# Moving transposed attention weights between partitions by DMAs through DRAM, in three vector operations a step and not in twelve

## The chip, the cores and the metric

The kernel runs on one core of a Trainium2 chip. The metric is the time of one execution on the device in microseconds (us), lower is better. Before the change the median of three runs is 905.54 us (904.55 to 905.82). Engines are named as in the profile: PE is TensorE (PEld its weight loads), DVE is VectorE, ACT is ScalarE, POOL is GpSimd, SP is SyncE, which here issues DMAs.

## The reference

Attention within a band of 64 keys, for 8 batches, 8 heads, 576 positions and 64 numbers a head, then a feed-forward layer over the 4608 tokens:

```python
scores = scale * np.matmul(q, k.transpose(0, 1, 3, 2))
mask = (rel >= 0) & (rel < window)          # rel = query - key, window = 64
scores = np.where(mask, scores, -1000000000.0)
attn = np.exp(scores - np.max(scores, axis=-1, keepdims=True))
attn = attn / (np.sum(attn, axis=-1, keepdims=True) + 1e-09)
x = np.matmul(attn, v)                      # then heads side by side: 4608 x 512
h = x @ w_in                                # 512 x 2048
g = np.where(h >= 1, h, np.where(h <= -1, 0.0, (h + 1) ** 2 / 4))
out = g @ w_out                             # 2048 x 512
```

## The kernel before

**Tiles and steps.** The tokens are worked off in nine tiles of 512. A tile's attention is four steps of 128 queries (steps 4t to 4t+3; from tile 2 on they are done in the order first, third, second, fourth, so step 8, 10, 9, 11). A step of the later kind is, for all eight heads at once: scores on PE (L409, 32 queries against the 96 keys that they can see), scale and mask on DVE (L426), maximum on DVE (L430), exponential on ACT (L437), sums turned over on DVE (L444, L445), division on DVE or POOL (L449), transposition of the weights on DVE (L455 in `att_transpose_both`), and the product with the values on PE (L484, `att_values`). Some steps' scores and an earlier step's values are issued as one piece.

**Why the transposition has twelve parts.** DVE transposes blocks of 32 x 32. The scores of 32 queries cover 96 keys, in three blocks of 32 columns. The product with the values needs keys on partitions, and the keys of the four groups of 32 queries start at different partitions; so each of 4 groups x 3 blocks is an operation of its own that reads 32 partitions and writes 32 others. The result lies in `ptd`, a buffer of which steps from `SOON` = 8 on use one copy (`pt2`): the next step's transpositions wait until this step's L484 is done. Steps below 8 do it in other ways (L464, or on PE by L470) and don't change.

**The feed-forward layer.** Weights are split in a high and a low part, and each product is made of three. Tiles 0 and 1 use the plain form: L873 for `x @ w_in` (groups of twelve matmuls for 128 columns of `w_in`), gates on ACT and DVE (L885, L890, L897, ACT L902, POOL L907), L924 for the second product (groups of twelve). From tile 2 on (`PLAIN`) the first product is formed from sums and differences of operand blocks, as L824, in chunks n = 0 to 7 of a tile with 24 and then 18 matmuls; DVE puts the pieces together (L840). It needs sums of the weights, which are made once during tile 1 on DVE and POOL (L734, L743, L753; ACT L265) and stored to DRAM (`kept`, L723, L758, L759), and from there loaded for each chunk into two pairs of ring buffers (`wr`, L796). It also needs sums and differences of a tile's x (the "build", two a tile: the copy L267 or L265 into `u`, four L537, five pairs of a rounding and L549).

**What sets the order.** `Plan` holds every piece of work with a key, a cost for each engine that may do it, what it comes after, and the buffers that it takes and gives back. It works through a timeline of its own: on each engine the piece that can start takes the next place, the lowest key first, and the instructions are issued in that order. So a changed cost or piece moves work on all engines. On the chip each engine works through its list in order and waits where a piece isn't ready. All loads and stores are issued by SP, in its list's order: ring loads, queries (`qt`), keys (`kt`), values (`vt`, four buffers), stores of sums and of the result (`out`, L955).

Of the kernel before, what the change touches and what calls it, by code (L numbers as in the profile page):

```python
# [10 lines left out]
F32 = mybir.dt.float32  # L11
F32R = mybir.dt.float32r
# [8 lines left out]
P = 128  # L21
QB = 64
SB = 2 * QB
WIN = 128
WINDOW = 64
SQ = 32
NEAR = WINDOW + SQ
# [12 lines left out]
SOON = 8  # L40
# [60 lines left out]
R_LEAD = 6  # L101
R_LOAD = 2800, 2100
A_EARLY = 5


class Plan:
# [87 lines left out]
def banded_attention_then_ffn(ctx: ExitStack, tc: tile.TileContext, q, k, v, w, masks, out, dims):  # L194
    nc = tc.nc
    B, H, S, D = dims
    NT, DM = out.shape
    NP = H // 2
# [25 lines left out]
    nmsk = const.tile([P, 3, WIN], F32, name="nmsk")  # L224
    idr = const.tile([P, P], F32R, name="idr")
    mskr = const.tile([P, 3, WIN], F32R, name="mskr")
    wpool = ctx.enter_context(tc.tile_pool(name="wpool", bufs=1))
    dram = ctx.enter_context(tc.tile_pool(name="dram", bufs=1, space=bass.MemoryType.DRAM))
    kept = [dram.tile([P, 2, 2, 7, P], F32, name=f"kept{n}") for n in range(NF // 2)]


    for n, at in ((P, QB), (QB, 0)):
        m = msk[:n, 0]
# [9 lines left out]
        nc.gpsimd.tensor_copy(msk[:, n], msk[:, 0])  # L243
        nc.gpsimd.memset(msk[r, n, :QB], NEG)

    ptq = const.tile([P, BUFS["ptd"], NP, SB], F32, name="ptd")
    ptd = [ptq[:, i] for i in range(BUFS["ptd"])]
    for t in ptd:
        nc.vector.memset(t, 0.0)

# [9 lines left out]
    add = plan.add  # L260
# [101 lines left out]
    blk, vals = {}, {}  # L362
    qts, kts, vts, pts = {}, {}, {}, {}
    starts = [sum(TILES[:t]) for t in range(len(TILES))]
    half = [slice(0, D), slice(D, P)]

    def pt_of(s, h):
        return h if s >= SOON else (2 * seq[s] + h) % len(ptd)

    def variant(s):  # L370
        firsts = [(2 * s + i) % NB == 0 for i in range(2)]
        return 1 if firsts[0] else 2 if firsts[1] else 0

    def near(s):
        return s >= PE_STEPS
# [12 lines left out]
        nc.sync.dma_start(out=t, in_=v[b * QB:b * QB + WIN])  # L388

    def load_masks():  # L390
        nc.sync.dma_start(out=nmsk[:, :, :NEAR], in_=masks)

    def round_masks():
        nc.scalar.copy(idr, idt)
        nc.scalar.mul(mskr[:, :2], msk[:, :2], 1.0 / scale)

    def att_scores(s, masked, pool):
        qt, kt = qts.pop(s), kts.pop(s)
# [21 lines left out]
    BOTH = slice(0, 2)  # L420

    def att_masked(s, h):
        ps, sm, _, _ = blk[s, h]
        m = nmsk[:, variant(s), :NEAR] if near(s) else msk[:, variant(s)]
        m = m.unsqueeze(1).broadcast_to(sm.shape)
        nc.vector.scalar_tensor_tensor(out=sm, in0=ps, scalar=scale, in1=m, op0=ALU.mult, op1=ALU.add)  # L426

# [20 lines left out]
        _, sm, _, den = blk[s, h]  # L448
        engine[eng].tensor_tensor(out=sm, in0=sm, in1=den.unsqueeze(2).broadcast_to(sm.shape), op=ALU.mult)  # L449

    def att_transpose_both(s, i, j, c):
        r = slice(i * QB + j * SQ, i * QB + (j + 1) * SQ)
        src = blk[s, BOTH][1][r].rearrange("p h a n -> p (h a) n")
        dst = ptq[(c + j) * SQ:(c + j + 1) * SQ, :2].rearrange("p h a n -> p (h a) n")
        nc.vector.transpose(dst[:, :, r], src[:, :, c * SQ:(c + 1) * SQ])  # L455

    def att_transpose(s, h, i):

# [15 lines left out]

    def att_values(s, pool):

        vt, pt = [vts.pop((s, i)) for i in range(2)], [ptd[pt_of(s, h)] for h in range(2)]
        vals[s] = ps = banks_of_heads(pool)
        for p in range(NP):
            for i in range(2):  # L480
                n = slice(i * QB, (i + 1) * QB)
                for h in range(2):
                    c = (2 * p + h) * D
                    nc.tensor.matmul(  # L484
                        ps[half[h], p, n], lhsT=vt[i][:, c:c + D], rhs=pt[h][:, p, n], start=True, stop=True
                    )

    def att_high(t, i, eng):
# [64 lines left out]
    early_values = []  # L553
    x_ready, x_first, x_after, seq = {}, {}, {}, {}
# [30 lines left out]
    def add_step(t, i):  # L585
# [44 lines left out]
        if s < SOON:  # L630
            for h in range(2):
                x = xs
# [30 lines left out]
        else:  # L663
# [478 lines left out]
```

## Time and profile before

| | |
|---|---|
| median of three runs | 905.54 us (904.55 to 905.82) |
| the profiled execution | 907.99 us, its span 906.2 us |
| mean granted clock of PE in it | 0.987 |
| DMA packets in it | 108033, 187.60 MB |
| DVE, transposition L455 | 336 operations, 146.5 us |
| SP waiting to issue ring loads (L796 for L824) | 426.1 us in 108 waits |

The page of the profile gives for each engine the time in which it was busy. PE's matmuls overlap, so a mean duration of one is longer than the pace at which they follow each other; groups in the timeline or in the chain show the pace. A view by stretches gives the busy times between two points in time, the view of waits who waited for whom (total, times, longest), the timeline the instructions of an engine in order, where [a <-b] is idle time ahead of a row and what ended it. The part of DMA issues gives the size of one and the median time from issue to landing.

### The profile page before, as it was taken

Reading aid. Unit: us, or ns where it says so; the run is one execution under the profiler, and the core shown is the slowest. Engines: PE = TensorE matmul, PEld = TensorE weight load, DVE = VectorE, ACT = ScalarE, POOL = GpSimd, SP = SyncE. Lnnn points to the kernel's source line nnn. Section 1 sums busy time; section 2 is a strip of 40 time slices with the busy share of each in tenths; the row PEclk is TensorE's granted clock in tenths of the full one; section 3 lists DMA queues with packets and bytes.
Section 4 is the critical chain, followed back from the end, with each engine's and each line's share of the span. In section 5 each row is a group of like instructions: output and inputs, shape, how many; then the busy total and the mean of one; then the engine's idle time right before and its main releaser. Section 6 shows DMA issues by size and latency. Waiting matters only on the chain.

```text
span 906.2 us, 20363 instructions
## 1 busy us (share of the span) xinstructions
PE 875.5 (97%) x7839; PEld 762.9 (84%) x7839; DVE 656.1 (72%) x1391; ACT 506.8 (56%) x1291; POOL 264.2 (29%) x268
## 2 busy tenths in 40 slices
PE   7699997999799999999999999999999999999998
PEld 5587885887688888888898889888988888899997
DVE  6999996598977868777686767676767676833331
ACT  7998863554455555655565537454655565434343
POOL 1000034455432232423142324232413242322222
PEclk9999996999899999999999999999999999999999
DMA  9991149447567666766676658666765664557531
GB/s 333 410 377 55 54 146 291 146 157 239 198 214 226 213 199 215 253 204 193 218 251 216 216 181 285 204 204 216 260 208 194 206 228 163 164 169 237 175 117 47
DMA packets 108033, 187.60 MB, mean 207 GB/s; under 512 B 8480, under 2 KB 49696, under 8 KB 107936
## 3 DMA queue, kind: packets, MB, share of 16 engines
q1 hardware_dynamic: 107648, 185.38, 60.9%
q8 instruction: 62, 1.02, 0.5%
q10 hardware_dynamic: 288, 0.92, 0.3%
q14 instruction: 35, 0.29, 0.1%
HBM read 162.15 MB, written 24.12 MB: 206 GB/s over the span
## 4 chain that ended last, share of the span: by engine, by line
PE 75%; DVE 12%; DMA 5%; ACT 3%; issue 2%; SPq 2%; POOL 0%; ACTq 0%; DVEq 0%
PE acc L924 36%; PE ps_h L824 27%; PE ps_h L873 6%; DVE ptd L455 4%; PE ps_a L484 3%; PE ps_a L409 3%; DVE a L897 2%; DMA kept<-half 2%; DMA kt<-in_k 2%; SPq L723 1%; ACT a L885 1%; DVE h L840 1%; DVE sm L449 1%; DVE half L734 1%; DVE half L743 1%
## 5 line engine op out<-in xcount | busy, mean ns | idle before, releaser
L924 PE MATMUL acc<-wts,gh 128*128 128x512 f32 x1154 | 363.2, 396 | 2.7 <-ACT o L265 2.7
L824 PEld LDWEIGHTS ps_h<-xs,wr 128*128 128x128 f32 x2352 | 294.5, 189 | 10.3 <-DVE h L840 0.7
L824 PE MATMUL ps_h<-xs,wr 128*128 128x256 f32 x2352 | 299.2, 282 | 0.3 <-DVE h L840 0.3
L907 POOL TENSOR_TENSOR gl<-a,gh 128x512 fp32r<-128x512 f32 (+1 forms) x130 | 167.6, 1290 | 427.5 <-ACT gh L902 389.7
L924 PEld LDWEIGHTS acc<-wts,gh 128*128 128x128 f32 x1154 | 207.9, 189 | 44.6 <-ACT o L265 3.4
L924 PE MATMUL acc<-wts,gl 128*128 128x512 f32 x577 | 225.9, 391 | 0.0
L840 DVE TENSOR_TENSOR h<-h,ps_h 128x256 f32<-128x256 f32 x280 | 117.5, 420 | 127.8 <-PE ps_h L824 113.0
L902 ACT CAST gh<-a 128x512 fp32r<-128x512 f32 (+1 forms) x149 | 90.0, 604 | 133.9 <-PE acc L924 112.2
L455 DVE STREAM_TRANSPOSE ptd<-sm 32x256 f32<-32x256 f32 x336 | 146.5, 436 | 6.3
L924 PEld LDWEIGHTS acc<-wts,gl 128*128 128x128 f32 x577 | 108.7, 188 | 23.9
L885 ACT ACTIVATE a<-h 128x512 f32<-128x512 f32 x112 | 69.9, 624 | 72.3 <-DVE h L840 71.4
L897 DVE SCALAR_TENSOR_TENSOR a<-a,h 128x512 f32<-128x512 f32 x112 | 85.7, 765 | 27.7 <-ACT a L890 16.2
L873 PE MATMUL ps_h<-xh,wts 128*128 128x512 f32 (+1 forms) x296 | 93.3, 385 | 10.7 <-DVE a L897 6.6
L437 ACT ACTIVATE sm<-sm,nm 128x96 f32<-128x96 f32 (+1 forms) x256 | 93.0, 365 | 12.2 <-DVE nm L430 12.1
L890 ACT ACTIVATE a<-a 128x512 f32<-128x512 f32 (+1 forms) x139 | 85.8, 617 | 4.3
L873 PEld LDWEIGHTS ps_h<-xh,wts 128*128 128x128 f32 x296 | 56.8, 200 | 22.6 <-DVE a L897 8.1
L873 PE MATMUL ps_h<-xl,wts 128*128 128x512 f32 (+1 forms) x148 | 56.3, 380 | 0.7 <-DVE xl L497 0.6
L265 ACT COPY h<-ps_h 128x256 f32<-128x256 f32 x77 | 28.7, 372 | 47.3 <-PE ps_h L824 43.6
L549 POOL TENSOR_TENSOR xs<-u,xs 128x256 fp32r<-128x256 f32 (+1 forms) x45 | 42.3, 971 | 32.0 <-ACT xs L265 32.0
L734 POOL TENSOR_TENSOR half<-wts 128x256 f32<-128x256 f32 x12 | 9.4, 790 | 140.1 <-PE ps_h L873 123.7
L437 ACT ACTIVATION_READ_ACCUMULATOR sm<-sm,nm 128x1 f32 x256 | 47.9, 187 | 0.0
L484 PEld LDWEIGHTS ps_a<-ptd,vt 128*64 128x64 f32 x992 | 32.0, 137 | 13.1 <-DVE ptd L455 3.6
(89 smaller groups left out, 728.3 us busy)
## 6 DMA issues: line engine op xcount, KB each, us to landing
wr<-kept SPq DMA_DIRECT2D x112, 512.0 KB, 4.7
wr<-kept SPq DMA_DIRECT2D x112, 384.0 KB, 3.9
vt<-in_v SPq DMA_DIRECT2D x72, 256.0 KB, 4.9
kt<-in_k SPq DMA_DIRECT2D x35, 384.0 KB, 5.4
raw<-in_w SPq DMA_DIRECT2D x12, 1023.8 KB, 10.3
qt<-in_q SPq DMA_DIRECT2D x36, 256.0 KB, 4.8
out<-o SPq DMA_DIRECT2D x33, 256.0 KB, 4.0
kept<-wts SPq DMA_DIRECT2D x48, 128.0 KB, 2.4
```

What stands on the lines that cost most here:

```text
L437: nc.scalar.activation(sm[:, p, :], (ps if masked else sm)[:, p, :], AF.Exp, bias=nm[:, p:p + 1], scale=scale if masked else 1.0, accum_ou ...
L455: nc.vector.transpose(dst[:, :, r], src[:, :, c * SQ:(c + 1) * SQ])
L484: nc.tensor.matmul(ps[half[h], p, n], lhsT=vt[i][:, c:c + D], rhs=pt[h][:, p, n], start=True, stop=True)
L824: nc.tensor.matmul(ps[:, c * 2 * SB:(c + 1) * 2 * SB], lhsT=r[:, part, cp, o], rhs=xo[k][:, xp, cp], start=i < 2 and c == 0 and j == 0 and ...
L840: nc.vector.tensor_tensor(out=h[:, to:to + 256], in0=h[:, of:of + 256], in1=ps[:, at:at + 256], op=ALU.add)
L873: nc.tensor.matmul(ps, lhsT=wts[f, 0][:, part, c * P:(c + 1) * P], rhs=x[:, c, r], start=(c == 0 and j == 0), stop=(c == NP - 1 and j == 2),)
L885: nc.scalar.activation(gs[t, f, r.start][0], phs[t, f, r.start], AF.Relu, bias=0.5, scale=0.5)
L890: nc.scalar.activation(a, a, AF.Square)
L897: nc.vector.scalar_tensor_tensor(out=a, in0=a, scalar=1.0, in1=ps, op0=ALU.min, op1=ALU.max)
L902: nc.scalar.copy(g[1], g[0])
L907: engine[eng].tensor_tensor(out=g[2], in0=g[0], in1=g[1].bitcast(F32), op=ALU.subtract)
L924: nc.tensor.matmul(acc[t, i][:, n], lhsT=g[:, sub], rhs=wts[f, 1][:, part, n], start=(q == 0 and j == 0), stop=(q == NF - 1 and j == 2 and ...
```

## The change

From step 8 on the weights are transposed by three operations over all 128 partitions, one for each block of 32 keys (`att_turn`), into `turned_at`: what comes out has, on partition 32g + k, the key k of block c of the query group g. One DMA writes that to a buffer in DRAM (`att_put`, 128 rows of 3 KB; `passed`, two of them, by the step's parity). Four DMAs, one for each group of 32 queries, read it back (`att_get`), each 96 rows of 1 KB to the 96 partitions of the keys that the group sees, into `seen`. `att_values` reads `seen`. The partitions of `seen` that a group doesn't see are cleared once, on POOL. The put waits for the transpositions; the gets wait for the put and for the values of the step before (`pt2`, as the transpositions did), `turned` is a buffer of one. In the plan the put costs SP 0.4 us and the gets 1.5, and their results count as there 3.5 us later. Two mask buffers lose parts that were not used.

```diff
-BUFS = dict(qt=2, kt=2, vt=4, ps_a=2, sm=2, ptd=3, pt2=1, x=2, u=2, ps_h=2, a=2, gh=2, gl=2, acc=4, o=2, h=2, ra=2, rb=2, tmp=2)
+BUFS = dict(qt=2, kt=2, vt=4, ps_a=2, sm=2, ptd=3, pt2=1, turned=1, x=2, u=2, ps_h=2, a=2, gh=2, gl=2, acc=4, o=2, h=2, ra=2, rb=2, tmp=2)
+MOVE = 400, 1500
+MOVE_LAG = 3500, 3500
...
+    passed = [dram.tile([P, NEAR // SQ, 2 * NP * SQ], F32, name=f"passed{n}") for n in range(2)]
...
+    MOVED = 2 * NP * SQ
+    ptq = const.tile([P, (4 + NEAR // SQ) * MOVED], F32, name="ptd")
+    seen = ptq[:, :4 * MOVED].rearrange("p (g m) -> p g m", m=MOVED)
+    turned_at = ptq[:, 4 * MOVED:].rearrange("p (c m) -> p c m", m=MOVED)
+
+    def clear_unseen():
+        nc.gpsimd.memset(seen[3 * SQ:, 0:3:2], 0.0)
+        nc.gpsimd.memset(seen[:SQ, 1:4:2], 0.0)
...
-    def att_transpose_both(s, i, j, c):
-        r = slice(i * QB + j * SQ, i * QB + (j + 1) * SQ)
-        src = blk[s, BOTH][1][r].rearrange("p h a n -> p (h a) n")
-        dst = ptq[(c + j) * SQ:(c + j + 1) * SQ, :2].rearrange("p h a n -> p (h a) n")
-        nc.vector.transpose(dst[:, :, r], src[:, :, c * SQ:(c + 1) * SQ])
+    def att_turn(s, c):
+        src = blk[s, BOTH][1].rearrange("p h a n -> p (h a) n")
+        nc.vector.transpose(turned_at[:, c].rearrange("p (m n) -> p m n", n=SQ), src[:, :, c * SQ:(c + 1) * SQ])
+
+    def att_put(s):
+        nc.sync.dma_start(out=passed[s % 2], in_=turned_at)
+
+    def att_get(s):
+        for g in range(SB // SQ):
+            j = g % (QB // SQ)
+            src = passed[s % 2][g * SQ:(g + 1) * SQ].rearrange("k c m -> c k m")
+            nc.sync.dma_start(out=seen[j * SQ:j * SQ + NEAR, g], in_=src)
...
+        if s >= SOON:
+            moved = seen.rearrange("p g (h a n) -> p g h a n", h=2, n=SQ)
+            pt = [lambda p, i, h=h: moved[:, 2 * i:2 * i + 2, h, p] for h in range(2)]
...
-            x += last["t"] + early_values
-            pieces_ = [(i, j, c) for i in range(2) for j in range(QB // SQ) for c in range(NEAR // SQ)]
-            for n, piece in enumerate(pieces_):
-                ends = n == len(pieces_) - 1
-                x = add(
-                    due, dict(DVE=440), lambda e, piece=piece: att_transpose_both(s, *piece),
-                    ready if ends else taken or x, takes=["pt2"] * (not n), gives=[("sm", xs)] * ends,
-                )
-                ready.append(x)
-                first = taken = taken or [x]
+            for c in range(NEAR // SQ):
+                ends = c == NEAR // SQ - 1
+                x = [add(
+                    due, dict(DVE=440), lambda e, c=c: att_turn(s, c), x + last["t"] * (not c),
+                    takes=["turned"] * (not c), gives=[("sm", xs)] * ends,
+                )]
+                if not c:
+                    [xt_] = x
+            x = [add(due, dict(SP=MOVE[0]), lambda e: att_put(s), x, gives=[("turned", xt_)], lag=MOVE_LAG[0])]
+            if s == SOON:
+                x.append(add(due, dict(Pool=900), lambda e: clear_unseen(), early_values))
+            x = add(due, dict(SP=MOVE[1]), lambda e: att_get(s), x, takes=["pt2"], lag=MOVE_LAG[1])
+            ready, first, taken = [x], [x], [x]
             gives = [("pt2", taken[0])]
```

The plan puts the whole program behind step 8 in another order. Three places of it follow; the numbers of lines are those of each kernel (in the changed one L464 is the transposition, L467 the put, L473 the gets, L419 the scores, L507 the values, L822 the ring loads, L850 the first product from tile 2 on, L923 the gate, L950 the second product).

First, DVE near the end of tile 1, where the second build of tile 2 (`u`, `xs`) stands. Before, its last rows and what comes behind them:

```order
L549 TENSOR_TENSOR xs<-u,xs 128x2x128
L743 TENSOR_TENSOR half<-half 128x128
L549 TENSOR_TENSOR xs<-u,xs 128x2x128
L444 TENSOR_SCALAR den<-den 128x8
L445 RECIPROCAL den<-den 128x8
L897 SCALAR_TENSOR_TENSOR a<-a,ps_h 128x512
L426 SCALAR_TENSOR_TENSOR sm<-ps_a,nmsk 128x384 x2
L753 TENSOR_TENSOR half<-half,o 128x512
```

Now, the last gate of tile 1 (L923) and the build's four sums (L560) behind it:

```order
L779 TENSOR_TENSOR half<-half,o 128x512
L464 STREAM_TRANSPOSE ptd<-sm 128x256 x2
L923 SCALAR_TENSOR_TENSOR a<-a,ps_h 128x512
L464 STREAM_TRANSPOSE ptd<-sm 128x256
L560 TENSOR_TENSOR u<-u 128x256 x4
L277 CAST xs<-u 128x2x2x128
L277 CAST xs<-u 128x2x128
L572 TENSOR_TENSOR xs<-u,xs 128x2x2x128 x2
```

Before, three gates of tile 1 (L897) stood behind that build; now none does, and no weight sum stands within it.

Second, PE at the first L824 of tile 2. Before, with L824 x30, two thirds of an L924 group at a time, and L824 x12 already ahead of these rows:

```order
L924 MATMUL acc<-wts,gl 128x512
L484 MATMUL ps_a<-ptd,vt 64x64 x16
L824 MATMUL ps_h<-xs,wr 128x256 x24
L409 MATMUL ps_a<-kt,qt 32x96 x32
L824 MATMUL ps_h<-xs,wr 128x256 x18
L924 MATMUL acc<-wts,gh 128x512 x2
```

Now, where the row L850 x12 is the first of its kind:

```order
L950 MATMUL acc<-wts,gl 128x512
L419 MATMUL ps_a<-kt,qt 32x96 x32
L850 MATMUL ps_h<-xs,wr 128x256 x12
L507 MATMUL ps_a<-ptd,vt 64x64 x16
L850 MATMUL ps_h<-xs,wr 128x256 x30
L419 MATMUL ps_a<-kt,qt 32x96 x32
L850 MATMUL ps_h<-xs,wr 128x256 x30
L950 MATMUL acc<-wts,gh 128x512 x2
```

Scores have moved ahead of the first product and values behind it; step 11's values stand two L950 groups and two scores ahead of the row L850 x12, where before four L924 groups, two L873 groups, scores of one step and values of another stood between them and the first L824.

Third, SP in a later tile (the numbers of the `kept` buffers, 93 to 100 before and 95 to 102 now, are chunks 0 to 7). Before:

```order
L796 DMA wr<-kept_93 128x2x512 x2
L796 DMA wr<-kept_93 128x2x384 x2
L796 DMA wr<-kept_94 128x2x512 x2
L388 DMA vt<-in_v 128x512 x2
L796 DMA wr<-kept_94 128x2x384 x2
L379 DMA qt<-in_q 128x512
L383 DMA kt<-in_k 128x768
```

Now:

```order
L822 DMA wr<-kept_95 128x2x512 x2
L467 DMA passed_93<-ptd 128x768
L822 DMA wr<-kept_95 128x2x384 x2
L473 DMA ptd<-passed_93 96x1x256 x4
L822 DMA wr<-kept_96 128x2x512 x2
L398 DMA vt<-in_v 128x512
L822 DMA wr<-kept_96 128x2x384 x2
L389 DMA qt<-in_q 128x512
L393 DMA kt<-in_k 128x768
```

The put and the gets stand between ring loads, with one pair of ring loads between them; behind a get that waits, the ring loads wait too.

More of the change, by code (lines that the diff above doesn't have):

```diff
@@ L244, in banded_attention_then_ffn @@
         nc.gpsimd.memset(msk[r, n, :QB], NEG)
-    ptq = const.tile([P, BUFS["ptd"], NP, SB], F32, name="ptd")
-    ptd = [ptq[:, i] for i in range(BUFS["ptd"])]
+    MOVED = 2 * NP * SQ
+    ptq = const.tile([P, (4 + NEAR // SQ) * MOVED], F32, name="ptd")
+    ptd = [ptq[:, i * NP * SB:(i + 1) * NP * SB].rearrange("p (a n) -> p a n", n=SB) for i in range(BUFS["ptd"])]
+    seen = ptq[:, :4 * MOVED].rearrange("p (g m) -> p g m", m=MOVED)
[3 more added lines that the diff above has]
+        nc.gpsimd.memset(seen[:SQ, 1:4:2], 0.0)
     for t in ptd:
@@ L367, in pt_of @@
     def pt_of(s, h):
[L368 removed]
+        return (2 * seq[s] + h) % len(ptd)
     def variant(s):
@@ L390, in load_masks @@
     def load_masks():
-        nc.sync.dma_start(out=nmsk[:, :, :NEAR], in_=masks)
+        nc.sync.dma_start(out=nmsk, in_=masks)
     def round_masks():
         nc.scalar.copy(idr, idt)
-        nc.scalar.mul(mskr[:, :2], msk[:, :2], 1.0 / scale)
+        nc.scalar.mul(mskr, msk[:, :2], 1.0 / scale)
     def att_scores(s, masked, pool):
@@ L423, in att_masked @@
         ps, sm, _, _ = blk[s, h]
-        m = nmsk[:, variant(s), :NEAR] if near(s) else msk[:, variant(s)]
+        m = nmsk[:, variant(s)] if near(s) else msk[:, variant(s)]
         m = m.unsqueeze(1).broadcast_to(sm.shape)
@@ L475, in att_values @@
     def att_values(s, pool):
-        vt, pt = [vts.pop((s, i)) for i in range(2)], [ptd[pt_of(s, h)] for h in range(2)]
+        vt = [vts.pop((s, i)) for i in range(2)]
+        if s >= SOON:
+            moved = seen.rearrange("p g (h a n) -> p g h a n", h=2, n=SQ)
+            pt = [lambda p, i, h=h: moved[:, 2 * i:2 * i + 2, h, p] for h in range(2)]
+        else:
+            pt = [lambda p, i, h=h: ptd[pt_of(s, h)][:, p, i * QB:(i + 1) * QB] for h in range(2)]
         vals[s] = ps = banks_of_heads(pool)
@@ L484, in att_values @@
                     nc.tensor.matmul(
-                        ps[half[h], p, n], lhsT=vt[i][:, c:c + D], rhs=pt[h][:, p, n], start=True, stop=True
+                        ps[half[h], p, n], lhsT=vt[i][:, c:c + D], rhs=pt[h](p, i), start=True, stop=True
                     )
```

4 lines of the change are left out of this document (2 added, 2 removed).

## The prediction

> **What bounds the kernel now.** I read the page first: the busy times and the chain that ended last.
>
> ```profile
> span 906.2 us, 20363 instructions
> PE 875.5 (97%) x7839; PEld 762.9 (84%) x7839; DVE 656.1 (72%) x1391; ACT 506.8 (56%) x1291; POOL 264.2 (29%) x268
> PE 75%; DVE 12%; DMA 5%; ACT 3%; issue 2%; SPq 2%; POOL 0%; ACTq 0%; DVEq 0%
> ```
>
> TensorE (PE) is idle for 906.2 - 875.5 = 30.7 us in all, and VectorE (DVE), which the change relieves, holds only 12% of the chain. So the question is not how much DVE work goes, but which of PE's idle time waits for DVE. The busy times by stretch of time (length, then PE, PEld, DVE, ACT, POOL, granted clock, DMA share, GB/s) place it.
>
> ```profile
> 140.00:160.00 20.00, 13.95 (x73) 11.07 (x68) 11.81 (x24) 8.04 (x28) 10.42 (x15) 0.66 1.00 313
> 143.30:146.50 3.20, 3.04 (x12) 2.75 (x13) 2.78 (x5) 0.00 (x0) 3.12 (x6) 0.50 0.84 228
> 220.00:240.00 20.00, 14.92 (x150) 11.60 (x149) 19.40 (x45) 10.70 (x32) 9.95 (x14) 0.97 0.79 263
> 240.00:245.00 5.00, 5.00 (x12) 3.86 (x13) 4.93 (x11) 2.15 (x4) 4.03 (x7) 0.50 0.28 109
> 273.00:367.00 94.00, 93.58 (x914) 83.40 (x913) 70.76 (x154) 50.80 (x143) 27.26 (x23) 1.00 0.67 218
> ```
>
> Tiles 2 to 8 take 94 us each, and in such a tile PE is busy for 93.58 us: nothing that DVE does there can be worth more than 0.42 us a tile. Behind step 8's start there are two holes. The one in 140 to 160 has DMA at a share of 1.00 and DVE at 11.81 of 20; the one in 220 to 240 has DVE at 19.40 of 20, and half a clock behind it. What PE waited for:
>
> ```profile
> PE ps_h L873 <- DVE a L897: 6.6, 3, 3.9
> PE ps_h L873 <- DVE xh L267: 4.1, 2, 2.6
> PE ps_a L484 <- DVE ptd L455: 2.5, 6, 0.4
> PE ps_a L484 <- DVE sm L426: 1.0, 1, 1.0
> ```
>
> The second row lies in the hole of 140 to 160. The 3.9 of the first, the 2.5 and the 1.0 can be reached. The timeline shows the 3.9:
>
> ```profile
> 227.67 1.51 PE L484 MATMUL ps_a<-ptd,vt 128*64 128x64 f32 x32 [1.04 <-DVE sm L426]
> 231.76 0.68 DVE L267 COPY u<-ps_a 128x512 f32<-128x512 f32 x1
> ...
> 238.40 0.41 DVE L549 TENSOR_TENSOR xs<-u,xs 128x256 fp32r<-128x256 f32 x1
> ...
> 239.05 0.64 DVE L897 SCALAR_TENSOR_TENSOR a<-a,ps_h 128x512 f32<-128x512 f32 x1
> 239.74 0.79 PE L873 MATMUL ps_h<-xh,wts 128*128 128x512 f32 x1 [3.90 <-DVE a L897]
> ```
>
> Step 11's values (227.67) release the second half of tile 2's build (L267 copy, L537, L549), 7.05 us of DVE rows from 231.76 to 238.81, and the gate L897 that frees a bank for the next L873 stands behind all of it. Then the clock is at 0.50, and a group of twelve L873 takes 5.49 where it normally takes 2.79, 2.7 lost:
>
> ```profile
> 239.74 5.49 PE ps_h L873 x12
> 108.61 2.79 PE ps_h L873 x12
> ```
>
> [...]
>
> **The change part by part.**
>
> ```profile
> L455 DVE STREAM_TRANSPOSE ptd<-sm 32x256 f32<-32x256 f32 x336 | 146.5, 436 | 6.3
> L464 DVE STREAM_TRANSPOSE ptd<-sm 32x128 f32<-32x128 f32 x24 | 7.3, 302 | 0.3
> ```
>
> Twelve L455 of 436 ns a step go, 28 steps, 146.5 us. Three of 128 partitions x 256 come in. No row has that shape; the two rows above say (436 - 302)/128 = 1.05 ns for each element of a partition, so I take 436 ns again; 4 x 436 would hold if the four groups of 32 partitions ran in turn. A step's DVE work falls from 5.2 to 1.3 us, in all by 110 us, nearly all from time in which PE worked.
>
> **The hole of 220 to 240.** In the new order on DVE the last L897 ahead of the L824 form stands before the four L537 of the second build, so that build holds no L873: -3.9 and -2.7. The wait of 1.0 at step 11's values goes with the transpositions that it came behind: -1.0. What is late next? Two things, both at the change to L824.
>
> ```profile
> 211.36 1.01 DVE L426 SCALAR_TENSOR_TENSOR sm<-ps_a,nmsk 128x384 f32<-128x384 f32 x2
> 221.51 0.43 DVE L455 STREAM_TRANSPOSE ptd<-sm 32x256 f32<-32x256 f32 x1
> ```
>
> ```profile
> SPq L758 <- ACT o L265: 33.8, 10, 8.3
> ```
>
> Step 11 takes 10.2 us from its scores to its first transposition in this crowded stretch, and the move below adds 10.3, at worst 11.9. In the new order 24.3 us of PE work lie between its scores and its values, so both fit, with 2.2 us left in the worse case. But its gets stand on SP behind two stores of weight sums, and SP waited up to 8.3 us for such a store; with 5 us of that, an estimate, the values come 2.9 late. Second, step 11's values stand only two L924 groups and two scores ahead of L824, 2 x 2.74 + 2 x 1.00 = 7.5 us, against the build's 7.05, which fits, or 9.6 if its copy comes as late as at 231.76 (2.6 behind the end of L484): 2.1 missing. The two waits together lie between 0 and 5 us; I take +2.0.
>
> **The move.** Put and gets are on SP:
>
> ```profile
> kept<-o SPq DMA_DIRECT2D x16, 256.0 KB, 2.4
> out<-o SPq DMA_DIRECT2D x33, 256.0 KB, 4.0
> vt<-in_v SPq DMA_DIRECT2D x72, 256.0 KB, 4.9
> kt<-in_k SPq DMA_DIRECT2D x35, 384.0 KB, 5.4
> 499.85 0.82 SPq L388 DMA_DIRECT2D vt<-in_v  x2
> ```
>
> A put is one write of 384 KB: between 2.4 and 4.0 us from issue to landing; I take 2.9, near the store to DRAM of the first row. Four gets of 96 KB: three issues of 0.41 ahead of the last (0.82 for two), and the last lands after 2.4 at best, 5.4 at worst; I take 4.9, the read that lies beside the same loads. With the three transpositions: 1.3 + 2.9 + 1.2 + 4.9 = 10.3 us, bounds 7.3 and 11.9. [...]
>
> Does the move fit? Pieces of a steady tile, and the way from scores to weights:
>
> ```profile
> 273.51 2.85 PE ps_h L824 x24
> 276.37 2.72 PE acc L924 x12
> 279.09 2.13 PE ps_h L824 x18
> 574.98 1.00 PE L409 MATMUL ps_a<-kt,qt 64*32 64x96 f32 x64
> 583.04 1.02 DVE L449 TENSOR_TENSOR sm<-sm,den 128x384 f32<-128x384 f32 x2
> 584.10 2.68 DVE L455 STREAM_TRANSPOSE ptd<-sm 32x256 f32<-32x256 f32 x6
> 592.92 1.04 PE L484 MATMUL ps_a<-ptd,vt 128*64 128x64 f32 x28 [0.42 <-DVE ptd L455]
> 551.22 1.02 DVE L426 SCALAR_TENSOR_TENSOR sm<-ps_a,nmsk 128x384 f32<-128x384 f32 x2 [0.49 <-PE ps_a L409]
> 559.72 1.03 DVE L449 TENSOR_TENSOR sm<-sm,den 128x384 f32<-128x384 f32 x2
> ```
>
> Scores end at 575.98, the weights are divided at 584.06: 8.1 us; the other step takes 551.2 to 560.75, 9.5. Before, three L924 groups, two L824 x24 and one x18 lie between scores and values, 16 us, and that just fails: the values wait 0.42. In the new order the four steps of a tile have 19.5, 19.9, 23.3 and 25.9 us of PE work there (a fourth L924 group, and six more L824 or another step's values, in the short two). Needed are 8.1 + 10.3 = 18.4, so the short ones have 1.1 and 1.5 to spare, and the six waits of 0.42 go: -2.5. With the slowest move (20.0) the short ones wait 0.5 and 0.1, 3.6 in six tiles; I take +1.2.
>
> SP itself has room: it spends its time waiting for ring buffers, and a ring load is issued some 20 us (two chunks less the L824 x24 that frees it) ahead of its use, while the reads above land in 5.4 at most. A put or get that holds SP for 2 to 4 us therefore delays loads that nobody waits for; it would cost from about 15 us on. 28 x 0.75 MB more on DMA engines with a share of 0.67 is hidden too. The clearing of unseen keys on POOL (two memsets, once) lies beside L873 work.
>
> **The hole of 140 to 160** has the same SP order up to step 8's put, and stays. One L743 of about 0.4 us now stands on DVE ahead of the xh copy that PE waits for there: between 0 and 0.8, I take +0.5.
>
> Sum: -7.6 - 2.5 + 2.0 + 1.2 + 0.5 = **-6.4 us**. The profiled execution took 907.99 us (span 906.2 and 1.8 around it) and becomes 901.6; the median of the three runs, 905.54, lies 2.45 lower, so I forecast **899.1 us**. With every gain and no cost it is 905.54 - 10.1 = 895.4, with every cost at its upper end (3.6 + 5 + 0.8) 904.8.
>
> **The rivals.**
> - *The idle time only changes its place.* Tile 2's build was the critical work at 231 to 239, and now PE reaches L824 earlier, so it may wait there, at L484 of step 11 or at the first L824, for what it gains. For it: the short 7.5 us. Against: DVE has 1.3 instead of 5.2 us a step, and in the new order none of the L743, L734 and L753 that stood between the build's rows before. Terms: -7.6 - 2.5 + 7 + 1.2 + 0.5, 904.1; I give 903.7 to 907.
> - *The move is longer than its gap: slower.* One mechanism, at L484 in every tile of the L824 form. It decides from a move of 11.4 us on (19.5 - 8.1). With 11.9 and the longer way of 9.5 the short steps wait 1.9 and 1.5, 3.4 a tile, 20 in six: 905.54 - 7.6 - 2.5 + 20 + 2 + 0.5 = 918. For it: reads beside ring loads land in 4.9 to 5.4, and the get is in runs of 1 KB. Against: the longer way was measured on a DVE that had four times the transpositions, and the slow case needs all ends at once.
> - *The transposition doesn't get cheaper*: 128 partitions cost 4 x 436 ns. DVE gains nothing, the move grows by 3.9 us, the short steps wait 2.8 and 2.4: 905.5 + 6 x 5.2 = 937. The two rows of different width speak against it.
> - *The early hole shrinks too*, if DVE's relief reaches the sums at 140 to 160: up to 5 us more, 890 to 895. DMA at 1.00 there speaks against it.
>
> **How the numbers follow.** Forecast 0.61, idle time moved 0.14, move too long 0.17, transposition no cheaper 0.02, early hole 0.06. The range from 894 to 909 leaves out most of the last three, about 0.2. About 0.2% (1.8 us) is what a measurement can tell here: faster means below 903.7. The forecast gives 0.59 of its 0.61 to that, the early hole 0.06, the moved idle time 0.01: 0.66 faster; 0.15 same; 0.19 slower.
>
> **What would show it.** Right: L464's new form near 436 ns; no wait of L873 for L897 beyond 230 us and clock 1.00 from 160 on; tiles of 93.6 to 94; L484 waiting under 0.3 us for DMA. Wrong: waits of L484 for the gets in every tile, of 1 us or more (second rival); a wait of several us at the first L824 (first rival); a tile longer than 94.4 us.

## The result and the profile after

The changed kernel takes 995.65 us (median of 4 runs, 993.75 to 997.66); the kernel before took 905.04 beside it (904.38 to 905.82). The ratio is 1.1001, with a 95% interval of 1.0976 to 1.1026: slower by a tenth, and far outside the range of 894 to 909. The page of the changed kernel, the lines that answer to those of before (span, busy times, granted clock of PE in 40 slices, DMA packets, chain by engine and by line):

```profile
span 992.0 us, 20313 instructions
PE 902.8 (91%) x7839; PEld 786.2 (79%) x7839; DVE 556.0 (56%) x1161; ACT 508.7 (51%) x1299; POOL 249.5 (25%) x240
PEclk8999998999989999999999999998999999999999
DMA packets 122897, 209.62 MB, mean 211 GB/s; under 512 B 8880, under 2 KB 60976, under 8 KB 122800
PE 53%; DMA 28%; SPq 7%; DVE 7%; ACT 2%; issue 2%; POOL 1%; ACTq 0%; POOLq 0%; DVEq 0%
PE acc L950 23%; DMA ptd<-passed 18%; PE ps_h L850 17%; PE ps_h L899 6%; DMA passed<-ptd 6%; SPq L473 5%; PE ps_a L507 4%; ACT sm L447 2%; DMA kt<-in_k 2%; PE ps_a L419 2%; DVE ptd L464 1%; DMA kept<-half 1%; DVE xs L572 1%; SPq L822 1%; DVE sm L459 1%
```

DVE is relieved by 100 us (656.1 to 556.0), as meant. But the chain that ended last has gone from PE to the move: 18% of it are the gets (`ptd<-passed`), 6% the put, 5% the issue of the gets on SP (L473). What PE waited for (total us, times, longest):

```profile
PE ps_a L507 <- DMA ptd<-passed: 56.5, 24, 3.0
PE ps_h L899 <- DVE xh L277: 5.7, 2, 4.5
PE ps_h L507 <- DMA ptd<-passed: 4.9, 2, 3.5
PE ps_h L899 <- DVE a L923: 2.6, 2, 2.1
```

The product with the values waits for the gets 26 times, in 24 of the 28 steps, 61.4 us in all, some 2.4 a time. The 3.9 us of the hole at 220 to 240 are gone (the longest wait for the gate L923 is 2.1). Two steps in the timeline, SP's list first (start, duration, line, what is moved, how many):

```profile
614.29 0.42 SPq L467 DMA_DIRECT2D passed<-ptd  x1
618.93 2.06 SPq L822 DMA_DIRECT2D wr<-kept  x2
621.08 2.94 SPq L473 DMA_DIRECT2D ptd<-passed  x4
...
669.02 0.33 SPq L467 DMA_DIRECT2D passed<-ptd  x1
669.79 0.90 SPq L822 DMA_DIRECT2D wr<-kept  x2
671.96 2.94 SPq L473 DMA_DIRECT2D ptd<-passed  x4
```

and PE at the values of the same steps:

```profile
631.30 1.04 PE L507 MATMUL ps_a<-ptd,vt 128*64 128x64 f32 x28 [2.94 <-DMA ptd<-passed]
632.27 4.63 PE L850 MATMUL ps_h<-xs,wr 128*128 128x256 f32 x24
...
671.76 3.02 PE L850 MATMUL ps_h<-xs,wr 128*128 128x256 f32 x24
...
681.31 1.76 PE L507 MATMUL ps_a<-ptd,vt 128*64 128x64 f32 x28 [2.84 <-DMA ptd<-passed]
```

From the first get's issue to the last one's landing, read as the end of PE's wait, it takes 631.30 - 621.08 = 10.2 us in the one step and 681.31 - 671.96 = 9.4 in the other, where the prediction had 1.2 + 4.9 = 6.1. The four issues take 2.94 us, 0.7 each, not 0.41. In the first step two ring loads stand on SP between put and gets and wait for their buffer, so the gets start 6.8 us behind the put; in the second it is 2.9. And behind these two waits PE is slow: in the first case 24 matmuls of L850 take 4.63 us, not 3.02, in the second the values take 1.76, not 1.04. Not every such wait is followed by a slower clock; the last section counts them.

Where the time goes is also seen at the two ends of L850 (L824 before): the last numbers are the starts of its first and its last matmul. Before, then after:

```profile
L824 PE MATMUL ps_h<-xs,wr x2352: 274/282/390, 254.8 to 891.3; 128*128 128x256 f32 x196
```

```profile
L850 PE MATMUL ps_h<-xs,wr x2352: 274/282/583, 258.0 to 977.1; 128*128 128x256 f32 x196
```

It begins 3.2 us later, and from first to last 636.5 us have become 719.1: the loss lies in the steady tiles, 82.6 us.

### The profile page after: what moved, and what is told of

Same layout as the page of the kernel before. It is cut to its first block, busy times and chain, and to the rows that moved or that the text cites. A ratio compares the mean times of both kernels' runs of the same rounds, so it can differ in the third digit from the quotient of the medians.

```text
span 992.0 us, 20313 instructions
## 1 busy us (share of the span) xinstructions
PE 902.8 (91%) x7839; PEld 786.2 (79%) x7839; DVE 556.0 (56%) x1161; ACT 508.7 (51%) x1299; POOL 249.5 (25%) x240
## 2 busy tenths in 40 slices
DMA packets 122897, 209.62 MB, mean 211 GB/s; under 512 B 8880, under 2 KB 60976, under 8 KB 122800
## 4 chain that ended last, share of the span: by engine, by line
PE 53%; DMA 28%; SPq 7%; DVE 7%; ACT 2%; issue 2%; POOL 1%; ACTq 0%; POOLq 0%; DVEq 0%
PE acc L950 23%; DMA ptd<-passed 18%; PE ps_h L850 17%; PE ps_h L899 6%; DMA passed<-ptd 6%; SPq L473 5%; PE ps_a L507 4%; ACT sm L447 2%; DMA kt<-in_k 2%; PE ps_a L419 2%; DVE ptd L464 1%; DMA kept<-half 1%; DVE xs L572 1%; SPq L822 1%; DVE sm L459 1%
## 5 line engine op out<-in xcount | busy, mean ns | idle before, releaser
L950 PE MATMUL acc<-wts,gh 128*128 128x512 f32 x1154 | 365.4, 398 | 0.0
L850 PEld LDWEIGHTS ps_h<-xs,wr 128*128 128x128 f32 x2352 | 306.9, 197 | 13.3 <-DVE h L866 3.6
L850 PE MATMUL ps_h<-xs,wr 128*128 128x256 f32 x2352 | 314.1, 290 | 3.0 <-DVE h L866 3.0
L933 POOL TENSOR_TENSOR gl<-a,gh 128x512 fp32r<-128x512 f32 (+1 forms) x130 | 170.7, 1315 | 434.2 <-ACT gh L928 381.6
L950 PEld LDWEIGHTS acc<-wts,gh 128*128 128x128 f32 x1154 | 210.6, 191 | 42.0 <-issue 0.4
L950 PE MATMUL acc<-wts,gl 128*128 128x512 f32 x577 | 227.2, 394 | 0.0
L950 PEld LDWEIGHTS acc<-wts,gl 128*128 128x128 f32 x577 | 109.7, 190 | 24.1
L923 DVE SCALAR_TENSOR_TENSOR a<-a,h 128x512 f32<-128x512 f32 x112 | 77.4, 691 | 40.8 <-ACT a L916 40.3
L507 PE MATMUL ps_a<-ptd,vt 128*64 128x64 f32 x992 | 46.8, 247 | 58.5 <-DMA ptd<-passed 56.5
L507 PEld LDWEIGHTS ps_a<-ptd,vt 128*64 128x64 f32 x992 | 39.4, 155 | 70.8 <-issue 60.1
L916 ACT ACTIVATE a<-a 128x512 f32<-128x512 f32 (+1 forms) x146 | 90.2, 618 | 4.6
L275 ACT COPY h<-ps_h 128x256 f32<-128x256 f32 x86 | 31.9, 371 | 49.1 <-PE ps_h L850 49.1
L572 POOL TENSOR_TENSOR xs<-u,xs 128x256 fp32r<-128x256 f32 (+1 forms) x32 | 33.2, 1055 | 93.5 <-DVE xs L277 54.0
L560 DVE TENSOR_TENSOR u<-u 128x256 f32<-128x256 f32 x53 | 20.2, 422 | 59.9 <-ACT u L275 58.2
```

The source lines that it names most:

```text
L507: nc.tensor.matmul(ps[half[h], p, n], lhsT=vt[i][:, c:c + D], rhs=pt[h](p, i), start=True, stop=True)
L850: nc.tensor.matmul(ps[:, c * 2 * SB:(c + 1) * 2 * SB], lhsT=r[:, part, cp, o], rhs=xo[k][:, xp, cp], start=i < 2 and c == 0 and j == 0 and ...
L916: nc.scalar.activation(a, a, AF.Square)
L923: nc.vector.scalar_tensor_tensor(out=a, in0=a, scalar=1.0, in1=ps, op0=ALU.min, op1=ALU.max)
L933: engine[eng].tensor_tensor(out=g[2], in0=g[0], in1=g[1].bitcast(F32), op=ALU.subtract)
L950: nc.tensor.matmul(acc[t, i][:, n], lhsT=g[:, sub], rhs=wts[f, 1][:, part, n], start=(q == 0 and j == 0), stop=(q == NF - 1 and j == 2 and ...
```

## The experiments

Theory A: a get is slow because the outermost dimension of what it reads is 3 (`"k c m -> c k m"`: three blocks of 32 rows), and therefore, as I suppose, few DMA engines work on it at a time. The rival B: a get is slow whatever its pattern, since it reads short rows from DRAM that were just written and stands behind ring loads. The rival C: its length doesn't matter by itself; the plan was told too short a time and placed the values too early.

**Plain rows (e1_rows).** A against B, with everything else left where it is.

```diff
-            src = passed[s % 2][g * SQ:(g + 1) * SQ].rearrange("k c m -> c k m")
+            src = passed[s % 2].rearrange("k c m -> (k c) m")[g * NEAR:(g + 1) * NEAR]
```

> One line of the gets: each reads 96 rows of 1 KB that stand one behind the other in the buffer, so its source is a plain 96 x 256 and no longer three blocks c of 32 rows with c outermost. Size, number and place of the DMAs, the list of every engine and all waits are those of the changed kernel. The rows moved are other ones than those that a group of queries needs, so the product with the values is formed from other weights. Theory A (the outermost dimension of 3 makes a get slow): a get's issue falls from 0.69 us to the 0.33 that the put takes, its landing from 6.2-7.3 us after the last issue to 3-5, the 28 waits of the values for the gets (61 us) all but vanish, and the kernel takes 895 to 915 us. Theory B (gets are slow because they stand behind ring loads in the queue, or read from DRAM what was just written, in 1 KB rows): nothing changes, 985 to 1000 us. [...]

Measured: 898.35 us, ratio 0.9911 (0.9878 to 0.9943). From its page: span, busy times, packets, and put and gets with their size and median us to landing:

```profile
span 897.3 us, 20313 instructions
PE 873.3 (97%) x7839; PEld 760.4 (85%) x7839; DVE 558.4 (62%) x1161; ACT 508.7 (57%) x1299; POOL 251.0 (28%) x240
DMA packets 124353, 209.63 MB, mean 234 GB/s; under 512 B 10336, under 2 KB 62432, under 8 KB 124256
passed<-ptd SPq DMA_DIRECT2D x28, 384.0 KB, 3.9
ptd<-passed SPq DMA_DIRECT2D x112, 96.0 KB, 3.5
```

What its values still wait for the gets, and the get's issue (min/median/max in ns):

```profile
PE ps_a L507 <- DMA ptd<-passed: 0.6, 2, 0.4
```

```profile
L473 SPq DMA_DIRECT2D ptd<-passed x112: 320/423/1627, 160.2 to 768.9; - x112
```

One line of the gets' pattern takes away the whole loss; B falls, since bytes, rows of 1 KB, queue and place in it are the same. The issue is 0.42 us and the landing 3.5, within the prediction's bounds of 2.4 to 5.4. It is not that the gets start sooner: read from SP's timeline, the first get is issued 4.9 us behind the put in the mean of the 28 steps, where it is 5.1 in the changed kernel. The step shown above with 6.8 has 6.1 here:

```profile
557.75 0.33 SPq L467 DMA_DIRECT2D passed<-ptd  x1
562.13 1.59 SPq L822 DMA_DIRECT2D wr<-kept  x2
563.82 1.90 SPq L473 DMA_DIRECT2D ptd<-passed  x4
```

The packets show what changed: 10336 - 8880 = 1456 more of under 512 bytes, 13 for each of 112 gets. And the trace of the changed kernel has the start and the duration of every packet, 46 ns in the median for one of 1 KB. The 384 packets of a step's four gets spread over 5.7 to 7.8 us in the 28 steps, and their durations add up to 2.6 to 3.2 times that: about three are under way at a time, and 384 / 3 x 46 ns is 5.9 us. The two stores of 128 KB at the end of the kernel, whose rows of 1 KB lie on 128 partitions, have 13.2 under way at a time, 256 packets in 0.91 us. No view here shows the single engines; that one engine stands behind each of the three is my reading.

These two kernels have the same lists of instructions on PE, so their difference can be split. PE's idle time is 992.0 - 902.8 = 89.2 us against 897.3 - 873.3 = 24.0, 65.2 less; its busy time is 902.8 against 873.3, 29.5 less. The mean granted clock is 0.960 in the one and 0.988 in the other. A third of the loss is thus the slower clock behind the waits, about 1.1 us for each of the 26 on average.

**Other outermost dimensions (a16_order, a8_order, a6_order, a4_order, a2_order).** The plain rows change two things, the outermost dimension and that rows stand one behind the other. These five read the same rows of a stretch in series, with the number of series outermost (16, 8, 6, 4, 2); the changed kernel is the case of 3. Where the expectations speak of engines, they count one for each unit of the outermost dimension up to 16. That is an assumption of mine; no run shows the engines.

```diff
-            src = passed[s % 2][g * SQ:(g + 1) * SQ].rearrange("k c m -> c k m")
+            rows = passed[s % 2].rearrange("k c m -> (k c) m")[g * NEAR:(g + 1) * NEAR]
+            src = rows.rearrange("(b a) m -> a b m", a=16)
```

> The changed kernel with the rows of a get read in another order: the same 96 rows of 1 KB of a stretch of the buffer, not one behind the other, but as 16 series of 6 (every sixteenth row), with 16 outermost. In the changed kernel it is 3 series of 32 (every third row), with 3 outermost. Other rows than the wanted ones reach a partition, so the product with the values takes other weights. If the count of the outermost dimension decides (16 DMA engines take part, not 3), it runs like the plain rows: 893 to 905 us, issue 0.42 us, landing 3.5. If it was that the rows stood one behind the other, it stays at 985 to 1000 us. In the packets: 13 small ones more for each of 112 gets, 1456 in all, as with the plain rows, by the first reading.

> As the run with 16 outermost, but with 8 outermost and 12 rows each. If the number of engines decides by degrees: 5 small packets more a get than the changed kernel (560 in all), the landing between 3.5 us and the 6.2 to 7.3 of three engines, nearer to the first (12 rows on an engine where three engines have 32 and sixteen have 6: some 4.2), and the issue still 0.69 us if that is what a get over fewer than 16 engines costs its queue. Then the move is some 2.5 us shorter than in the changed kernel, the waits of 2.2 us are nearly gone, and the time is 898 to 925 us. If only 16 helps, it stays above 970.

> The rows of a get as 6 series of 16, 6 outermost; other rows than the wanted ones reach a partition. A straight line through what was seen (32 rows an engine: the values go on 6.4 to 7.3 us behind the last issue; 6 rows: landing 3.3) gives 0.135 us for each row on an engine, so 16 rows land some 2.1 us earlier than 32. The wait of the changed kernel is 2.2 us a step: under 0.3 is left, 898 to 915 us, 3 small packets more a get than there (336). If the loss hangs on less than 8 engines by a step and not by degrees, over 960.

> 4 outermost, 24 rows each, otherwise as the run with 6. By the same line the gets land 1.1 us earlier than in the changed kernel, and half of the wait of 2.2 us a step is left: 1.1 x 28 = 31 us and as much of the clock's part as such short waits still cost, 925 to 955 us; 112 small packets more than the changed kernel.

> 2 outermost, 48 rows each, otherwise as the run with 6. By the same line the gets land 2.2 us later than in the changed kernel; the waits double to some 4.4 us a step, 61 us more, and with the clock's part (29 us in the changed kernel) 1055 to 1100 us; 112 small packets fewer than the changed kernel. If the gap and not the engines set the loss, it stays within 10 us of 995.

| outermost | rows a small packet | small packets | issue, us | values wait for gets, us | median, us | ratio (95%) |
|---|---|---|---|---|---|---|
| 2 | 48 | 8768 | 0.62 | 112.3 | 1072.53 | 1.183 (1.178 to 1.188) |
| 3 (the change) | 32 | 8880 | 0.69 | 61.4 | 995.65 | 1.100 (1.098 to 1.103) |
| 4 | 24 | 8992 | 0.61 | 18.9 | 929.76 | 1.026 (1.022 to 1.029) |
| 6 | 16 | 9216 | 0.71 | 5.9 | 910.11 | 1.004 (1.002 to 1.006) |
| 8 | 12 | 9440 | 0.66 | 2.3 | 901.39 | 0.995 (0.992 to 0.997) |
| 16 | 6 | 10336 | 0.59 | 0.5 | 901.30 | 0.993 (0.991 to 0.996) |
| 96 (plain rows) | 6 | 10336 | 0.42 | 0.6 | 898.35 | 0.991 (0.988 to 0.994) |

(The rows for each small packet of a get are 96 divided by the outermost dimension, at most 16; the case of 2 has two runs.) The numbers of small packets are exact: 112 for each unit of the outermost dimension up to 16, and 96 has as many as 16. From the pages with 2, 8 and 16:

```profile
DMA packets 122785, 209.62 MB, mean 196 GB/s; under 512 B 8768, under 2 KB 60864, under 8 KB 122688
```

```profile
DMA packets 123457, 209.62 MB, mean 233 GB/s; under 512 B 9440, under 2 KB 61536, under 8 KB 123360
```

```profile
DMA packets 124353, 209.63 MB, mean 233 GB/s; under 512 B 10336, under 2 KB 62432, under 8 KB 124256
```

So it is the count, and not that rows are contiguous. It goes by degrees: from 8 series on the waits for the gets are 2.3 us or less, and below that the fewer series, the longer the values wait. All five times fell into the ranges expected, though the waits came out smaller than the straight line of landing over rows had them (18.9 us with 4 series where it gave 31, 51 more with 2 where it gave 61). One part of my reading was wrong: the issue doesn't go with the count. It is 0.59 us for 16 series and 0.61 for 4, against 0.42 for plain rows; it goes with the form of the pattern, and why is open.

**The right rows, laid out for the gets (e2_layout, v6_gets, e2_plan).**

```diff
-    passed = [dram.tile([P, NEAR // SQ, 2 * NP * SQ], F32, name=f"passed{n}") for n in range(2)]
+    passed = [dram.tile([SB // SQ, NEAR // SQ, SQ, 2 * NP * SQ], F32, name=f"passed{n}") for n in range(2)]
...
-        nc.sync.dma_start(out=passed[s % 2], in_=turned_at)
+        for g in range(SB // SQ):
+            dst = passed[s % 2][g].rearrange("c k m -> k c m")
+            nc.sync.dma_start(out=dst, in_=turned_at[g * SQ:(g + 1) * SQ])
...
-            src = passed[s % 2][g * SQ:(g + 1) * SQ].rearrange("k c m -> c k m")
+            src = passed[s % 2][g].rearrange("c k m -> (c k) m")
```

> The buffer in DRAM is laid out by group, block, key. So a group's 96 rows stand one behind the other and a get reads a plain 96 x 256; the put becomes four DMAs of 32 partitions each, with 32 outermost. The right rows are moved; PE, DVE, ACT and POOL have the lists of the changed kernel, SP issues three DMAs a step more (84 x some 0.35 to 0.7 us, of which SP has room). Theory A: gets land as in the run with plain rows; the puts' issue takes 1.4 to 2.8 us and not 0.33, so the move takes some 1 to 2 us longer than there; 900 to 925 us. Theory B: 985 to 1005 us.

Measured: 899.72 us, ratio 0.9921 (0.9901 to 0.9941). It does all the work of the kernel before, and it is 0.8% faster than that kernel and a tenth faster than the changed one. From its page, and its stretches of time:

```profile
span 895.8 us, 20435 instructions
PE 871.4 (97%) x7839; PEld 759.3 (85%) x7839; DVE 557.7 (62%) x1161; ACT 508.7 (57%) x1299; POOL 249.8 (28%) x240
passed<-ptd SPq DMA_DIRECT2D x112, 96.0 KB, 2.9
ptd<-passed SPq DMA_DIRECT2D x112, 96.0 KB, 3.8
```

```profile
140.00:160.00 20.00, 15.36 (x95) 13.07 (x96) 9.25 (x21) 8.57 (x28) 8.55 (x13) 0.83 0.98 297
220.00:240.00 20.00, 20.00 (x112) 16.16 (x112) 15.32 (x29) 13.57 (x46) 11.54 (x17) 1.00 0.79 265
```

```profile
L852 PE MATMUL ps_h<-xs,wr x2352: 274/282/388, 248.0 to 880.8; 128*128 128x256 f32 x196
```

PE is busy throughout 220 to 240, at full clock. The first product of tile 2 begins at 248.0, 6.8 us earlier than before, and from its first to its last matmul it takes 632.8 us, 3.7 less; these are single executions, and with plain rows, where PE has the same list, the two numbers are 250.1 and 632.3.

The same with one put and six gets, each for one block and one half, 32 partitions outermost:

```diff
+        rows = passed[s % 2].rearrange("(i j k) c m -> j c k i m", j=QB // SQ, k=SQ)
+        for j in range(QB // SQ):
+            for c in range(NEAR // SQ):
+                nc.sync.dma_start(out=seen[(j + c) * SQ:(j + c + 1) * SQ, j::QB // SQ], in_=rows[j, c])
```

> The layout of the changed kernel, one put a step, and six gets in place of four: one for each block c and half j, which reads 32 partitions x 2 groups x 256 with 32 outermost. All rows are the right ones. SP issues 7 DMAs a step, where the other layout has 8. Put 2.9 us, six issues of 0.42 = 2.5, landing 3.5: 8.9 us with the transposition's last part left out, where the other layout has 1.8 + 2.9 + 1.8 + 3.8 = 10.3 from first issue to last landing. If the move is inside the gap in both, the times agree within 0.3% (896 to 902 us).

Measured: 900.96 us, ratio 0.9928 (0.9904 to 0.9952). And the layout by group with `MOVE = 1700, 1700` and `MOVE_LAG = 2500, 3500`:

> The layout by group with what it costs told to the plan: 1.7 us of SP for the four puts and 1.7 for the four gets, results 2.5 and 3.5 us behind. The plan orders the program anew. If what is left of the waits is not the move's, it stays within 0.4% of 899.7 us (896 to 903); if puts that the plan thought shorter still push other pieces back, it falls to 890 to 896.

Measured: 900.28 us, ratio 0.9916 (0.9895 to 0.9938). The three can't be told apart. Once the outermost dimension of the gets is 32 or 96, neither the number of DMAs nor the plan's figures for them makes a difference that these intervals show.

**DVE's relief alone (e4_three).**

```diff
-            pieces_ = [(i, j, c) for i in range(2) for j in range(QB // SQ) for c in range(NEAR // SQ)]
+            pieces_ = [(0, 0, c) for c in range(NEAR // SQ)]
```

> The kernel before, with three of a step's twelve transpositions and the other nine left out (the product with the values then reads what an earlier step left on the other partitions). It has no move. This is what the relief of DVE alone would be worth: 252 operations of 436 ns fewer, 110 us of DVE time. My prediction's terms for it are -7.6 (the hole at 220-240 us) and -2.5 (six waits of steady tiles): 893 to 900 us. If DVE's work was what PE waits for in more places than I read, it falls below 890; if it was hidden throughout, it stays within 2 us of 905.

Measured: 897.31 us, ratio 0.9898 (0.9862 to 0.9933). So DVE's relief alone, in the order that the plan gives it, is worth about 9 us of 906, as forecast. The layout by group reaches 0.9921, so its move is hidden but for what these intervals can't resolve.

**The true length told to the plan (e3_lag).** Theory C, with the slow gets left in.

```diff
-MOVE = 400, 1500
-MOVE_LAG = 3500, 3500
+MOVE = 400, 2900
+MOVE_LAG = 3000, 7500
```

> The changed kernel with the move's true length told to the plan: 2.9 us of SP for the four gets and their result 7.5 us later (before 1.5 and 3.5), the put's 3.0 later. The DMAs are those of the changed kernel, the plan orders all engines anew and can place other matmuls ahead of the values. If the loss is the wait alone and the plan can fill it (theory C), the 28 waits of some 2.2 us shrink to under 0.5 and the time falls to 900 to 925 us with gets as slow as before. If nothing else stands ready for PE, the wait goes to another row and it stays over 960.

Measured: 928.06 us, ratio 1.025 (1.0212 to 1.0287). Its waits for the gets, and the ends of L850:

```profile
PE ps_a L507 <- DMA ptd<-passed: 6.0, 3, 2.6
```

```profile
L850 PE MATMUL ps_h<-xs,wr x2352: 274/282/583, 264.8 to 909.8; 128*128 128x256 f32 x196
```

Three waits are left, so three quarters of the loss can be planned away with gets that are as slow as before. It still isn't as good as the kernel before: L850 begins 10.0 us later than there and takes 645.0, 8.5 more. Between 240 and 280, at the change to L850, its PE is busy for 28.9 of 40 us, in these stretches:

```profile
240.00:260.00 20.00, 14.86 (x180) 10.55 (x180) 14.69 (x30) 12.07 (x54) 6.14 (x9) 1.00 0.63 222
260.00:280.00 20.00, 14.02 (x165) 12.38 (x166) 8.04 (x20) 7.08 (x25) 3.60 (x4) 0.61 0.62 210
```

All three waits for the gets that are left lie in this stretch (0.96, 2.59 and 2.43 us). And L850 itself waits there for the operands that the build makes of the values, and goes on slower: its next 22 matmuls take 4.69 us, where 24 took 3.02 in the changed kernel, and the clock of 260 to 280 is 0.61:

```profile
264.80 0.79 PE L850 MATMUL ps_h<-xs,wr 128*128 128x256 f32 x2 [0.60 <-DVE xs L277]
267.20 4.69 PE L850 MATMUL ps_h<-xs,wr 128*128 128x256 f32 x22 [1.61 <-POOL xs L572]
```

C is a part of the truth: the plan's figure decides what a slow move costs in the steady tiles, where no wait for the gets is left, but at that change the slow gets still cost time.

**The gets directly behind the put on SP (s1_sp).**

```diff
+    fetched, used = [], []
     def att_put(s):
         nc.sync.dma_start(out=passed[s % 2], in_=turned_at)
+        if s > SOON and len(fetched) == len(used):
+            att_get(s)
     def att_get(s):
+        if s in fetched:
+            return
+        fetched.append(s)
```

> The changed kernel with the gets of a step (from the second on) directly behind its put in SP's list; PE, DVE, ACT and POOL have their lists unchanged, and the gets are the slow ones with 3 outermost. In the changed kernel one or two ring loads stand between, which wait for a buffer, and the first get is issued 2.6, 6.6, 5.2 to 6.8 and 4.2 us behind the put in the four steps of a tile. If that costs, 4, 3 and 1.6 us come off three of four steps, their waits of 2 to 3 us fall to 0, 0 and 0.7, and only the step that has 2.6 already keeps its 2.3 to 2.8: some 22 us of waits in place of 61, and with the clock's part (29 us for 61) 935 to 945 us. Then the wait of all four steps, which I had given to the two short ones only, is explained by the place in SP's list on top of the slow gets. If the slow gets alone explain it, nothing changes: 985 to 1000 us. Holding SP for the put should cost nothing at the ring loads.

Measured: 998.91 us, ratio 1.1029 (1.0977 to 1.1081): a miss. What PE waited for, then SP (L515 is the product with the values there, L480 the gets):

```profile
PE ps_a L515 <- DMA ptd<-passed: 34.2, 20, 3.1
PE ps_a L515 <- DVE sm L436: 15.2, 5, 4.2
PE ps_h L515 <- DMA ptd<-passed: 6.7, 3, 3.2
```

```profile
SPq L480 <- DMA passed<-ptd: 100.6, 27, 8.7
```

The waits for the gets fall from 61.4 to 40.9 us, but 15.2 come back at the mask (L436) that frees the values' bank. In those steps the mask stands on DVE behind the copy of a result into `o`:

```profile
398.40 0.69 DVE L277 COPY o<-acc 128x512 f32<-128x512 f32 x1 [4.95 <-DMA out<-o]
503.96 0.69 DVE L277 COPY o<-acc 128x512 f32<-128x512 f32 x1 [5.14 <-issue]
```

In the changed kernel these two copies wait 0.29 and 0.16 us, for the store of `o`; here the store stands on SP behind put, gets and ring loads. For the first of them the view names the store itself, so I take it for what the others wait for too; no run took it away alone. Also, SP waits 100.6 / 27 = 3.7 us for a put on average and up to 8.7: more of the gets' delay is the put itself, and less SP's list, than I had read from one tile. The first get is still issued 4.2 us behind the put in the mean, 0.9 less than in the changed kernel.

## Why the prediction was wrong

**The step that failed** is in the paragraph on the move: "Four gets of 96 KB: three issues of 0.41 ahead of the last (0.82 for two), and the last lands after 2.4 at best, 5.4 at worst; I take 4.9". All of the rows behind it are transfers with 128 partitions outermost. The gets have 3, as the added line says (`"k c m -> c k m"` with c = 3), and a get with 3 outermost has no row in the trace of before. It took 9.4 to 10.2 us for issue and landing, where the upper bound was 1.2 + 5.4. With 96 outermost the same bytes took three issues of 0.42 and a landing of 3.5 to 3.8, 4.8 to 5.1 us, where I had taken 6.1 and the bounds were 3.6 and 6.6: the estimate held for the transfer that I had in mind.

**The rival "the move is longer than its gap"** (0.17, 918 us) is what happened. Its mechanism and its place, at the values in nearly every step, were right; its price was 20 us, and 82.6 were lost in the steady tiles. I had the two short steps of a tile wait, 1.9 and 1.5 us; 24 of 28 steps wait, 2.4 us a time. Besides the gets, a second term was too small: I took 2.9 us from the put to the gets, and it is 5.1 in the mean, since the put lands after 3.9 us (plain rows) and ring loads stand between. That term alone costs next to nothing: with plain rows it is 4.9, and the values wait 0.6 us in all. And I gave the waits no clock, though in the prediction's row of 143.30 to 146.50, behind a wait of 2.6 us for L267, the clock is at 0.50: 29.5 of the 94.7 us are that.

**"SP has room"** held for the loads: PE waits for no ring load, neither in the changed kernel nor with plain rows. It did not hold for SP's stores in the last experiment.

**The terms of the sum** can be read in the run with the layout by group, where the move is what I took it for. The hole of 220 to 240 is gone, as forecast; in place of the six waits for L455 (2.5 us) there are two for the gets, 0.8 us in all. L464 in its new form takes 417 ns (436 forecast):

```profile
L464 DVE STREAM_TRANSPOSE ptd<-sm 128x256 f32<-128x256 f32 x84 | 31.6, 417 | 0.3
```

Up to the first product of tile 2 the terms -7.6, +2.0 and +0.5 make -5.1; it was -6.8. In the steady tiles -2.5 and +1.2 make -1.3; it was -3.7. The hole of 140 to 160, which I let stay, shrank a little (PE busy 15.36, not 13.95; clock 0.83, not 0.66), as it did in the changed kernel (15.24 and 0.83). These terms are read too large: the two profiled executions differ by 10.4 us, the medians of the two kernels by 6.4. The forecast of 899.1 us is 0.9929 of 905.54, and that kernel measures 0.9921 (0.9901 to 0.9941). So the sum came out for a change that is one pattern away from this one; its single terms are confirmed only as far as single executions can tell, within some 4 us.

**The range** failed with the bound of the gets. A bound from the nearest rows holds only if the unknown operation is of their kind; here the pattern was not, and it was written in the diff.

## What to carry to other kernels

Look at the outermost dimension of both patterns of every DMA that a change adds: here gets of the same 96 KB gave 929.76 to 1072.53 us with 2 to 4 outermost in their source, and 898.35 with 96. Lay the buffer in DRAM out so that it isn't small on either side; here 32 outermost in the puts and 96 in the gets turned a tenth lost into 0.8% gained (995.65 us, then 899.72). And price waits of 2 us and more on PE with their clock: here that was half as much again on average, 29.5 us for 61.4 us of waits.

## What the runs showed of the hardware

- The number of small packets of a get follows its outermost dimension exactly, 2, 3, 4, 6, 8, 16, and stops at 16: from 8768 to 10336 in all, 112 for each unit with 112 gets, and 10336 again with 96 outermost.
- Waits of PE of 2 to 3 us can be followed by the half clock, but their length alone doesn't decide. Of the 22 waits for the gets of 2.0 to 3.0 us in the changed kernel, 13 have a lower granted clock in the 3 us behind them (0.50 to 0.76), and 9 have 1.00. A wait of 2.99 us is among the 9, one of 2.05 among the 13 (the two rows, then the 3 us behind each; the number ahead of the last two is the clock):

```profile
436.66 1.03 PE L507 MATMUL ps_a<-ptd,vt 128*64 128x64 f32 x28 [2.99 <-DMA ptd<-passed]
601.44 1.23 PE L507 MATMUL ps_a<-ptd,vt 128*64 128x64 f32 x28 [2.05 <-DMA ptd<-passed]
436.66:439.66 3.00, 3.00 (x45) 2.93 (x46) 1.28 (x4) 1.14 (x3) 0.00 (x0) 1.00 0.46 139
601.44:604.44 3.00, 3.00 (x32) 2.53 (x33) 1.10 (x3) 1.74 (x8) 0.00 (x0) 0.61 1.06 404
```

In the kernel before, the clock is at 0.50 behind a wait of 2.6 us (143.30 to 146.50) and behind one of 3.90 (240 to 245). So a wait of 2 to 3 us must be counted with its clock on average, 29.5 us for the 26 waits, and not each time.

- A get's issue on SP costs 0.42 us for plain rows and 0.59 to 0.71 for rows in series with 2 to 16 outermost, in no order of that number.
